# Value products of two heads on the column halves of the array, in an attention, SwiGLU and GELU kernel on one core

## The chip, the core and the metric

The kernel runs on one core of one Trainium2 chip. The metric is the device time of one execution in microseconds (us). TensorE (PE) multiplies, VectorE (DVE), ScalarE (ACT) and GpSimd (POOL) work on tiles, SyncE (SP) issues most transfers. PE multiplies tiles of float32r with one pass over the columns of the moving operand; a float32 product ("exact" here) is issued as one instruction and appears in the trace as two records.

## The reference

Causal attention with a bias from a cumulative sum, then a SwiGLU block and a GELU block (x·sigmoid(1.702x)) on the 2304 tokens.

```
B, H, S, D = 4, 8, 576, 64
scores = q @ k.T / sqrt(D) + min(-(cum_i - cum_j), 0), causal      # cum = cumsum(max(s, 0))
attn = softmax(scores)                                             # sum + 1e-9 below the line
x = (attn @ v) as (2304, 512)
xn = x / sqrt(mean(x*x) + 1e-6) * rms_g
x = (silu(xn @ w_gate) * (xn @ w_val)) @ w_out                     # 512 -> 1536 -> 512
out = gelu(x @ w_in) @ w_out2                                      # 512 -> 2048 -> 512
```

The weights come as 8-byte floats and are decoded on the chip.

## The kernel before

**Attention.** There are 32 heads (4 batches of 8), each with 576 queries and keys in five blocks. `scores` multiplies a head in six pieces of 192, 64, 320, 448, 288 and 288 columns (1600 in all). For the heads in `QF` (0 to 9) each piece is one float32 product of the tiles `QS` and `KS`. For the others the pair of heads is split into high and low halves (`prep`: round, subtract, seven small transfers a head), and each piece is two float32r products (`QA`·`KA`, `QB`·`KB`). DVE adds the mask and takes the row maximum, ACT takes the exponential (`expo`), POOL multiplies by the reciprocal of the row sum (`norm`). `transp` turns the probabilities in four PSUM tiles of 320, 512, 512 and 512 columns; they are copied to the SBUF tiles `PT`. `pv` multiplies them with the values: piece 0 of three products (320, 256, 128 columns), piece 1 of five (four of 256, one of 128), 1856 columns a head.

**The value product.** For the heads in `VF` (0 to 9) `pv` issues one float32 product per part, whose stationary tile `VS` holds the values of both heads of a pair, 128 columns; only the 64 output rows of the head at hand are copied out, to `xT`. For the other 22 heads each of the four `PT` tiles is kept twice, as a rounded copy (`hi`, by ACT) and the rest (`lo`, a DVE subtraction), and each part is two float32r products with a stationary tile of 64 high and 64 low value columns. The two halves of the output are then added (ACT copies one to `BT`, DVE adds).

**What else runs there.** After each batch `rms` takes the row norms: twenty products of a 128-column stationary tile with two columns, then six transposes, of which three have only 64 rows and so use half of the array's rows. Between the heads PE gets "fill": four of the twelve SwiGLU chunks for tokens of batches that are done (`fa_tile`, 256 columns a product, three float32r products for each exact one). When attention ends the rest of SwiGLU and GELU follows, a chain of products of 384 and 512 columns (`Group`, `Down`), to the end.

**The order.** The kernel records all operations, lays them in time with a planner (costs per operation, due times `HD`, `FD`, `WD`, `TA`), lets it choose the engine where an operation names several ("AV": ACT or DVE), and fixes the order on every engine at build time. At run time each engine goes through its list and waits where an input is late. Seven products of no use (`IDLE`) stand at the start.

Of the kernel before, what the change touches and what calls it, by code (L numbers as in the profile page):

```python
# [10 lines left out]
F32 = mybir.dt.float32  # L11
# [12 lines left out]

PRM = {
    "G0": 4, "NWS": 17, "NWO": 12, 
    "QF": set(range(10)), "VF": set(range(10)),
    "TIN": [(t * 256, 256) for t in range(6)],
    "PPB": 3, "PTB": 8, "XHB": 7, "HHB": 5,
    "VIRT": 260096,  # L30
    "SLOTS": {
# [5 lines left out]
    },  # L37
# [8 lines left out]
    "TA": 227.54, "REB": 3, "PASS": 0, "ISSUE": 0.45, "IDLE": 7, "PEN": {},  # L46
}


# [1 line left out]
def attention_then_swiglu_then_gelu(ctx: ExitStack, tc, qT, kT, vp, s, w1, w2, gT, out):  # L51
# [6 lines left out]
    NC2 = w2.shape[0]  # L58
    HB = B * H
    G0 = PRM["G0"]  # L60
    QF, VF = PRM["QF"], PRM["VF"]
    TIN = PRM["TIN"]
    TS = max(n for _, n in TIN)
    TA = sum(n for _, n in TIN)
# [35 lines left out]
    def few(n):  # L100
# [6 lines left out]
    RY = [few(5) for _ in range(2)]  # L107

    SHAPE = {
        "Q": [S], "K": [S], "mask": [S], "SQ": [S], "VS": [5, 2 * D], "PA": [1600], "PT": [512], "VP": [2, 5, 2, D],  # L110
        "BT": [320], "XH": [2, TS], "TH": [TS], "FH": [2, TS], "YO": [2, TS], "w": [2, 512], "wb": [512], "ws": [512],
        "MK": [2, 2, H2], "HH": [2, H2], "M5": [H2], "SG": [H2], "V1": [H2], "RE": [H2], **{nm: [2, 2, H2] for nm in NAMES},
    }
    ROUND = ("QA", "QB", "KA", "KB", "VP", "XH", "FH", "w", "HH", *NAMES)

    def stem(name):
        for k in (name, name[:2], name[:1]):
            if k in SHAPE:
                return k
# [29 lines left out]
    for slot, lists in PRM["SLOTS"].items():  # L149
        k = 0  # L150
        for x, names in enumerate(lists):
            names = names.split()
            if names[0].startswith("PT"):
                if VF:
                    place(slot, k, names, False)
                    k += 1
                place(slot, k, names, True)
            else:
                kind = stem(names[0])
                place(slot, k, names, names[0][:2] in ROUND or kind in ROUND)  # L160
            k += 1
        WIDE[slot] = max(hi - lo for lo, hi, t, _, _ in turns if t == slot)
    starts = [t[0] for t in turns]

    def get(name, n=None):
        if n is None:
            return BUF[name][0]
        return [BUF[f"{name}{i}"][0] for i in range(n)]

    QS, KS, QB, KB, QA, KA, VS, BT, TH = (get(x, 2) for x in ("QS", "KS", "QB", "KB", "QA", "KA", "VS", "BT", "TH"))  # L170
    VTP = get("VP")
    VT = [VTP[:, 0], VTP[:, 1]]
    mask, SQ, SQT, YO = (get(x) for x in ("mask", "SQ", "SQT", "YO"))
    PA = get("PA", NB)
    XH, FH = get("XH", PRM["XHB"]), get("FH", PRM["HHB"])
    PT = {f: [BUF[f"PT{i}"][0 if f else -1] for i in range(PRM["PTB"])] for f in ((True, False) if VF else (False,))}
    WS = [own(f"w{i}", [2, 512], F32R) for i in range(PRM["NWO"])] + [BUF[f"w{i}"][0] for i in range(PRM["NWO"], NWS)]
    PC = {nm: BUF[nm][0] for nm in NAMES}
    MK, HH, M5, SG = get("MK", 2), get("HH", 8), get("M5", 2), get("SG", 2)
# [195 lines left out]
    def sub(o_, x, y, **kw):  # L375
        tt(o_, x, y, ALU.subtract, **kw)
# [21 lines left out]
    def decode(unit, dst):  # L398
        i = unit_i[0]
        unit_i[0] += 1  # L400
        st = ST[i % 2]
        which, c, u = unit
        dma(st, (w1 if which == "1" else w2)[c, :, u, :], after=first_score[:1] if i < 2 else ())
        hw = st.bitcast(I32).rearrange("p (n t) -> p n t", t=2)[:, :, 1]
        lw = st.bitcast(U32).rearrange("p (n t) -> p n t", t=2)[:, :, 0]
        li = st.bitcast(I32).rearrange("p (n t) -> p n t", t=2)[:, :, 0]
        mi, ai = wm.bitcast(I32), dst.bitcast(I32)
        op("A", lambda e: e.activation(out=li, in_=lw, func=AF.Copy, scale=2.0 ** -29), cost=0.68)
        op("V", lambda e: e.tensor_scalar(
            out=mi, in0=hw, scalar1=0x7FFFFFFF, scalar2=None, op0=ALU.bitwise_and), cost=0.43)  # L410
        op("G", lambda e: e.tensor_scalar(
            out=wm, in0=wm, scalar1=E_MAX, scalar2=E_MIN, op0=ALU.min, op1=ALU.max), cost=0.63)
        op("V", lambda e: e.tensor_scalar(
            out=mi, in0=mi, scalar1=3, scalar2=0x3FFFFFFF, op0=ALU.logical_shift_left, op1=ALU.bitwise_and), cost=0.43)
        op("V", lambda e: e.scalar_tensor_tensor(
            out=ai, in0=hw, scalar=-0x40000000, in1=mi, op0=ALU.bitwise_and, op1=ALU.bitwise_or), cost=0.69)
        op("G", lambda e: e.tensor_tensor(out=ai, in0=ai, in1=li, op=ALU.add), cost=1.3)
# [10 lines left out]


    hd = {}  # L430
    pt_i, bt_i, xh_i, fh_i, th_i = [0], [0], [0], [0], [0]

    def turn(bufs, i):
        i[0] += 1
# [53 lines left out]
    def prep(h):  # L488
# [9 lines left out]
        else:  # L498
# [7 lines left out]
            for t, c0, x in ((QA, 0, qh), (KA, 0, kh), (KA, 64, kh), (QA, 64, ql), (QB, 0, qh), (KB, 0, kl)):  # L506
                dma(t[i][c0:c0 + 64, :].bitcast(F32), x)
            dma(KB[i][64:66, :].bitcast(F32), ch_d[h])
        if h not in VF and i == 0:
            src = VS[h // 2 % 2].rearrange("p k (h d) -> p h k d", h=2)  # L510
            rnd(PRM["RV"], VTP[:, :, :, 0, :], src)
            sub(VTP[:, :, :, 1, :], src, VTP[:, :, :, 0, :])

    PO = [576, 640, 832, 1152]

# [54 lines left out]

    def norm(h, qb):
        pt, rc = p_of(h, qb), RC[h % NB]
        op(PRM["NORM"], lambda e: e.tensor_scalar(
            out=pt, in0=pt, scalar1=rc[:, qb:qb + 1], scalar2=1.0, op0=ALU.mult, op1=ALU.mult))

    TP = [
# [7 lines left out]
    def transp(h, t):  # L584
# [8 lines left out]

        op("T", fn)
        n = TCOLS[t]
        hi = turn(PT[h in VF], pt_i)
        if h in VF:
            def fn(e):
                if e.tag == "A":
                    e.activation(out=hi[:, :n], in_=ps[:, :n], func=AF.Copy, scale=1.0)  # L600
                else:
                    e.tensor_copy(out=hi[:, :n], in_=ps[:, :n])

            op("AV", fn)
            hd[h, t] = (hi,)
        else:
            lo = turn(PT[False], pt_i)
            cp(hi[:, :n], ps[:, :n])
            tt(lo[:, :n], ps[:, :n], hi[:, :n], ALU.subtract, eng="V")
            hd[h, t] = (hi, lo)  # L610

    PVP = [
        (0, 320, [(0, 0, 0, 0, 320), (1, 0, 1, 64, 256), (2, 0, 2, 192, 128)]),
# [2 lines left out]
    ]  # L616

    def pv(h, piece, due):
        b_, hh = divmod(h, H)
        f32 = h in VF  # L620
        q0, n, parts = PVP[piece]
        ps = bank(h, "v", 2 * h + piece)
        r0 = 64 * (hh % 2)
        t0 = b_ * S + q0
        xo = xT[r0:r0 + 64, hh // 2, t0:t0 + n]
        for i, (t, c, kb, oc, w) in enumerate(parts):
            def fn(e, i=i, t=t, c=c, kb=kb, oc=oc, w=w):
                if f32:
                    e.matmul(ps[:, oc:oc + w], VS[h // 2 % 2][:, kb, :], hd[h, t][0][:, c:c + w],
                             start=i == 0, stop=i == len(parts) - 1)  # L630
                else:
                    for j in range(2):
                        e.matmul(ps[:, oc:oc + w], VT[h % 2][:, kb].rearrange("p a d -> p (a d)"),
                                 hd[h, t][j][:, c:c + w], start=i == 0 and j == 0, stop=i == len(parts) - 1 and j == 1)

            op("T", fn)
        if f32:
            def fn(e):
                if e.tag == "A":
                    e.activation(out=xo, in_=ps[r0:r0 + 64, :n], func=AF.Copy, scale=1.0)  # L640
                else:
                    e.tensor_copy(out=xo, in_=ps[r0:r0 + 64, :n])

            op("AV", fn, due=due, g=f"h{h}")
            return
        bt = turn(BT, bt_i)
        cp(bt[0:64, :n], ps[64:P, :n])
        tt(xo, ps[0:64, :n], bt[0:64, :n], ALU.add, eng="V", due=due, g=f"h{h}")

# [134 lines left out]
    for h in range(HB):  # L784
# [7 lines left out]
            norm(h, qb)  # L792
        for t in range(4):
            transp(h, t)
        pv(h, 0, PRM["HD"][h])
        pv(h, 1, PRM["HD"][h])
        b_, hh = divmod(h, H)
        if hh % 2:
            rms_sq(b_, hh // 2)
        if hh == H - 1:  # L800
# [326 lines left out]
    n = 0  # L1127
# [322 lines left out]
```

## Time and profile before

| | |
|---|---|
| median of 3 runs | 1039.67 us (1037.95 to 1040.34) |
| the profiled execution, device time | 1040.27 us |
| its span, first to last instruction | 1038.5 us |
| PE busy | 1022.5 us, 98% |
| DVE, ACT, POOL busy | 697.6, 569.3, 407.1 us |
| mean granted clock | 0.995 |

Every instruction has the line L212 of a helper, so the rows are told apart by tiles. A name as `b<-sg,s 128x256` reads: written to PSUM (b), from the moving tile in slot sg and the stationary in slot s, 256 columns. The length of a PE record includes the way through the array and overlaps the next; what an instruction takes from PE is the distance from its start to the next start. The names of slots: sf, sg, sh hold `PT`, sb the split values, s_0_141 the exact `QS` and `KS`.

### The profile page before, as it was taken

To read this page: it belongs to the slowest core of one execution; us is meant where nothing else is said; L and a number is where in the kernel's file an instruction comes from. 1 tells how busy PE (TensorE), PEld (TensorE's weight loads), DVE (VectorE), ACT (ScalarE), POOL (GpSimd) and SP (SyncE) were. 2 spreads that over 40 slices of the span, in tenths; PEclk is the share of its full clock that TensorE was granted. 3 is DMA by queue.
4 is the path that set the end of the run, shared out by engine and by line. 5 is a ranking of instruction groups with operands and counts; after the bars stand their busy time and mean duration, and the time that the engine had idled before them with its cause. 6 is when DMAs were issued, how large, how long until landed. Compare 5 with 4: busy or idle time off the path is not lost.

```text
span 1038.5 us, 17144 instructions
## 1 busy us (share of the span) xinstructions
PE 1022.5 (98%) x6070; PEld 960.2 (92%) x6070; DVE 697.6 (67%) x1573; ACT 569.3 (55%) x1299; POOL 407.1 (39%) x472
## 2 busy tenths in 40 slices
PE   9998999999999999999999999999999999999998
PEld 5877999999999999999999999988999988999987
DVE  6767888877978775787744787876663475473333
ACT  5876786877785445454432444666663344453322
POOL 5666875776563632353300444632330042030000
PEclk9998999999999999999999999999999999999999
DMA  5448665675414745574543277665175136514541
GB/s 153 119 119 198 157 164 148 156 199 139 114 46 132 264 145 190 193 270 157 208 178 122 80 290 279 264 244 233 62 281 196 66 104 255 213 41 158 206 183 61
DMA packets 63037, 176.19 MB, mean 170 GB/s; under 512 B 7220, under 2 KB 24116, under 8 KB 62952
## 3 DMA queue, kind: packets, MB, share of 16 engines
q1 hardware_dynamic: 62840, 175.02, 50.5%
q8 instruction: 48, 0.79, 0.3%
q14 instruction: 37, 0.30, 0.1%
q10 hardware_dynamic: 112, 0.08, 0.0%
HBM read 111.34 MB, written 44.26 MB: 150 GB/s over the span
## 4 chain that ended last, share of the span: by engine, by line
PE 95%; DMA 1%; DVE 1%; SPq 1%; issue 0%; ACT 0%; POOL 0%; DVEq 0%; ACTq 0%
PE b L212 95%; SPq L212 1%; DMA s<-s 1%; DMA s<-in_kT_dram 0%; DVE s L212 0%; DMA s<-in_qT_dram 0%; DVE xT L212 0%; POOL sg L212 0%; DVE sd L212 0%; ACT s L212 0%; ACT sg L212 0%; DVE sh L212 0%; DVE wa L212 0%; ACT sa L212 0%; DVE small L212 0%
## 5 line engine op out<-in xcount | busy, mean ns | idle before, releaser
L212 PE MATMUL b<-s,w 128*128 128x384 f32 x930 | 177.6, 334 | 0.0
L212 PEld LDWEIGHTS b<-s,w 128*128 128x128 f32 x930 | 163.0, 188 | 0.6
L212 POOL TENSOR_TENSOR wa<-wa,st 128x512 int32<-128x512 int32 x52 | 72.9, 1402 | 197.0 <-ACT sb L212 60.8
L212 DVE TENSOR_TENSOR xT<-b,xT 128x384 f32<-128x384 f32 (+1 forms) x134 | 80.3, 609 | 86.5 <-PE b L212 85.5
L212 PE MATMUL b<-sc,w 128*128 128x256 f32 (+1 forms) x744 | 122.5, 301 | 0.0
L212 ACT ACTIVATE b<-b 128x384 f32<-128x384 f32 x119 | 55.8, 480 | 95.8 <-DVE b L212 56.7
L212 PEld LDWEIGHTS b<-sc,w 128*128 128x128 f32 x744 | 106.5, 192 | 0.9 <-issue 0.2
L212 PE MATMUL b<-sd,w 128*128 128x384 f32 (+1 forms) x594 | 107.3, 312 | 0.1
L212 PE MATMUL b<-s 128*128 128x288 f32 (+5 forms) x398 | 92.8, 359 | 7.8 <-DMA s<-in_kT_dram 2.5
L212 POOL TENSOR_SCALAR wm<-wm 128x512 f32<-128x512 f32 x68 | 47.1, 693 | 134.8 <-DVE wm L212 125.8
L212 POOL TENSOR_SCALAR s<-s,small 128x576 f32<-128x576 f32 (+4 forms) x160 | 89.5, 577 | 21.5 <-DVE small L212 10.8
L212 PEld LDWEIGHTS b<-sd,w 128*128 128x128 f32 x594 | 92.7, 189 | 0.8 <-DVE sd L212 0.3
L212 ACT ACTIVATE s<-s,small 128x576 f32<-128x576 f32 (+4 forms) x160 | 88.3, 554 | 7.7 <-DVE small L212 7.2
L212 PE MATMUL b<-s,s 128*128 128x384 f32 (+1 forms) x453 | 91.1, 338 | 0.0
L212 PEld LDWEIGHTS b<-s 128*128 128x128 f32 x398 | 63.0, 198 | 19.3 <-issue 9.0
L212 PEld LDWEIGHTS b<-s,s 128*128 128x128 f32 x453 | 79.6, 188 | 1.2
L212 DVE CUSTOM_DVE_ANT_0 s<-b,s 128x192 f32<-128x192 f32 (+4 forms) x160 | 64.3, 424 | 19.5 <-PE b L212 18.9
L212 PE MATMUL b<-ident,s 128*128 128x128 f32 x480 | 73.1, 277 | 1.3 <-POOL s L212 0.7
L212 PE MATMUL b<-w,sc 128*128 128x512 f32 x270 | 74.2, 390 | 0.0
L212 ACT ACTIVATE sa<-b 128x384 f32<-128x384 f32 (+1 forms) x100 | 45.0, 452 | 47.6 <-DVE b L212 26.9
L212 ACT ACTIVATE se<-b 128x384 f32<-128x384 f32 (+2 forms) x82 | 38.3, 469 | 58.8 <-PE b L212 52.2
L212 ACT ACTIVATE st<-st 128x512 int32<-128x512 uint32 x68 | 45.8, 674 | 40.3 <-DMA st<-in_w_dram 40.0
(152 smaller groups left out, 2183.6 us busy)
## 6 DMA issues: line engine op xcount, KB each, us to landing
st<-in_w_dram SPq DMA_DIRECT2D x68, 512.0 KB
s<-s SPq DMA_DIRECT2D x132, 144.0 KB
s<-pc21B SPq DMA_DIRECT2D x9, 768.0 KB
xT<-y_d SPq DMA_DIRECT2D x3, 1536.0 KB
s<-pc11B SPq DMA_DIRECT2D x6, 768.0 KB
s<-pc22B SPq DMA_DIRECT2D x6, 768.0 KB
out_dram<-xT SPq DMA_DIRECT2D x18, 256.0 KB
s<-in_vp_dram SPq DMA_DIRECT2D x16, 256.0 KB
```

What stands on the lines that cost most here:

```text
L212: return lambda *args, **kw: f(*[real(x) for x in args], **{k: real(x) for k, x in kw.items()})
```

## The change

- `pv` is called once per pair of heads. It issues, for each part, one float32 product for each head, each with 64 value columns, placed on columns 0 to 63 and 64 to 127 of the array (`tile_position`). Both write the same PSUM bank, one the lower, one the upper 64 partitions, and one copy of 128 partitions takes both to `xT`. This goes for all 32 heads; the rounded and rest copies of `PT`, the split of the values (`VP`) and the additions (`BT`) are gone. `PT` has 12 tiles in place of 8.
- `QF` has heads 0 to 13, so four more heads have exact scores.
- The planner may give the normalising to ACT or GpSimd (the table still says GpSimd), and one step of the weight decoding (`mag`) to ACT as well as DVE.
- New due times and a planner's cost for a piece of `pv`.

```
-    "QF": set(range(10)), "VF": set(range(10)),
+    "QF": set(range(14)),
-    "PPB": 3, "PTB": 8, "XHB": 7, "HHB": 5,
+    "PPB": 3, "PTB": 12, "XHB": 7, "HHB": 5,
-    "TA": 227.54, "REB": 3, "PASS": 0, ...
+    "TA": 129.28, "REB": 3, "EARLY": False, "MAG": "AV", "PASS": 0, ..., "PVC": (1.4, 2.1),
...
-        op("V", lambda e: e.tensor_scalar(
-            out=mi, in0=hw, scalar1=0x7FFFFFFF, scalar2=None, op0=ALU.bitwise_and), cost=0.43)
+        def mag(e):
+            if e.tag == "A":
+                e.activation(out=wm, in_=hw.bitcast(F32), func=AF.Abs)
+            else:
+                e.tensor_scalar(out=mi, in0=hw, scalar1=0x7FFFFFFF, scalar2=None, op0=ALU.bitwise_and)
+        op("AV", mag)
...
-        if h in VF:
...
-            op("AV", fn)
-            hd[h, t] = (hi,)
-        else:
-            lo = turn(PT[False], pt_i)
-            cp(hi[:, :n], ps[:, :n])
-            tt(lo[:, :n], ps[:, :n], hi[:, :n], ALU.subtract, eng="V")
-            hd[h, t] = (hi, lo)
+        pt = turn(PT, pt_i)
...
+        op("AV", fn)
+        hd[h, t] = pt
...
-                if f32:
-                    e.matmul(ps[:, oc:oc + w], VS[h // 2 % 2][:, kb, :], hd[h, t][0][:, c:c + w],
-                             start=i == 0, stop=i == len(parts) - 1)
...
+        def fn(e):
+            for i, (t, c, kb, oc, w) in enumerate(parts):
+                for j in range(2):
+                    r0 = 64 * j
+                    e.matmul(ps[r0:r0 + 64, oc:oc + w], VS[h // 2 % 2][:, kb, r0:r0 + 64], hd[h + j, t][:, c:c + w],
+                             start=i == 0, stop=i == len(parts) - 1, tile_position=(0, r0))
+        op("T", fn, cost=PRM["PVC"][piece])
...
-        bt = turn(BT, bt_i)
-        cp(bt[0:64, :n], ps[64:P, :n])
-        tt(xo, ps[0:64, :n], bt[0:64, :n], ALU.add, eng="V", due=due, g=f"h{h}")
...
-        pv(h, 0, PRM["HD"][h])
-        pv(h, 1, PRM["HD"][h])
+        if hh % 2:
+            for piece in range(2):
+                pv(h - 1, piece, PRM["HD"][h // 2])
```

How the order moves, at three places. PE, a piece 0 of the value product among transposes (`ident`) and fill (`sc` by `w`), one of the 22 split heads before:

```order
L212 MATMUL b_69<-ident,s_0_151 128x128 x4
L212 MATMUL b_72<-sc_929,w_130 128x256 x6
L212 MATMUL b_70<-sf_1047,sb_992 128x320 x2
L212 MATMUL b_70<-sf_1047,sb_992 128x256
L212 MATMUL b_70<-sg_1089,sb_992 128x256
L212 MATMUL b_72<-sc_929,w_130 128x256 x3
L212 MATMUL b_70<-sg_1089,sb_992 128x128 x2
```

The same place after, a pair of heads (the slots sa and sb now hold `PT` tiles too):

```order
L204 MATMUL b_69<-ident,s_0_138 128x128 x4
L204 MATMUL b_72<-sc_910,w_129 128x256 x6
L204 MATMUL b_70<-sb_389,s_0_151 64x320
L204 MATMUL b_70<-sf_260,s_0_151 64x320
L204 MATMUL b_70<-sb_389,s_0_151 64x256
L204 MATMUL b_70<-sf_260,s_0_151 64x256
L204 MATMUL b_70<-sb_389,s_0_151 64x128
L204 MATMUL b_70<-sf_260,s_0_151 64x128
```

A piece is now one unbroken stretch of instructions that alternate between the halves; over the whole list there are 256 of them in 31 stretches, with full-array products before and after each.

DVE, before, between the heads of the split kind (the subtractions into sf and sg, the split of the values into sb, the addition of `BT` from sa):

```order
L212 TENSOR_TENSOR sf_1047<-b_68,sf_1047 128x320
L212 SCALAR_TENSOR_TENSOR se_987<-se_987,b_72 128x256
L212 TENSOR_SCALAR sb_992<-s_0_146 128x10x64
L212 TENSOR_TENSOR se_987<-se_987,b_72 128x256
L212 TENSOR_TENSOR sb_992<-s_0_146,sb_992 128x10x64
L212 TENSOR_TENSOR sg_1089<-b_69,sf_1047 128x512
L212 TENSOR_TENSOR xT<-b_70,sa_1127 64x256
L212 TENSOR_TENSOR sg_1089<-b_68,sg_1089 128x512
```

After, at the like place:

```order
L204 SCALAR_TENSOR_TENSOR se_983<-se_983,b_72 128x256
L204 TENSOR_TENSOR se_983<-se_983,b_72 128x256
L204 COPY xT<-b_70 128x320
L204 COPY sf_260<-b_68 128x320
L204 ISA s_0_138,small<-b_66,s_0_147 128x192
L204 ISA small 128x1
```

Copies, shared between DVE and ACT, stand where subtractions, splits and additions stood.

PE at the very start, before (`128x512` are the products of no use, s_0_141 the exact scores):

```order
L212 MATMUL b_72<-s_0_151 128x512 x6
L212 MATMUL b_66<-s_0_141 128x192
L212 MATMUL b_66<-s_0_141 128x64
L212 MATMUL b_73<-s_0_141 128x288
L212 MATMUL b_71<-s_0_141 128x448
```

After:

```order
L204 MATMUL b_72<-s_0_168 128x512
L204 MATMUL b_66<-s_0_141 128x192
L204 MATMUL b_66<-s_0_141 128x64
L204 MATMUL b_73<-s_0_141 128x288
L204 MATMUL b_71<-s_0_141 128x448
L204 MATMUL b_67<-s_0_141 128x320
L204 MATMUL b_66<-s_0_141 128x288
L204 MATMUL b_72<-s_0_168 128x512 x2
```

One product of no use stands ahead of the first head instead of six; the rest are spread between the first heads.

## Rows read from the trace of the kernel before

**Rows 1.** The page: busy time; the granted clock in 40 slices.

```profile
PE 1022.5 (98%) x6070; PEld 960.2 (92%) x6070; DVE 697.6 (67%) x1573; ACT 569.3 (55%) x1299; POOL 407.1 (39%) x472
...
PEclk9998999999999999999999999999999999999999
```

**Rows 2.** Busy time by stretch: start, attention with fill, the chain behind it.

```profile
core 0: us, PE busy (x) PEld busy (x) DVE busy (x) ACT busy (x) POOL busy (x), PEclk, DMA share, GB/s
0.00:100.00 100.00, 91.53 (x466) 71.82 (x467) 68.86 (x238) 67.82 (x191) 63.40 (x99) 0.96 0.54 148
100.00:340.00 240.00, 237.29 (x1893) 231.81 (x1893) 198.46 (x582) 178.59 (x464) 157.45 (x216) 1.00 0.53 140
340.00:1038.50 698.50, 693.63 (x3715) 656.59 (x3713) 430.30 (x755) 322.87 (x646) 186.26 (x158) 1.00 0.50 183
```

**Rows 3.** Waits of PE, longest first: us in total, times, longest.

```profile
PE b L212 <- DMA s<-in_kT_dram: 2.5, 1, 2.5
PE b L212 <- DVE s L212: 2.0, 1, 2.0
PE b L212 <- DMA s<-s: 2.0, 2, 1.3
```

**Rows 4.** Timeline of PE (start, us, operation): exact value product of one head.

```profile
51.26 1.14 PE L212 MATMUL b<-sf,s 128*128 128x320 f32 x4
...
53.96 0.38 PE L212 MATMUL b<-sf,s 128*128 128x128 f32 x2
54.18 0.60 PE L212 MATMUL b<-ident,s 128*128 128x128 f32 x4
54.62 0.39 PE L212 MATMUL b<-sf,s 128*128 128x128 f32 x2
54.84 1.19 PE L212 MATMUL b<-s 128*128 128x288 f32 x4
```

**Rows 5.** Timeline of PE: pieces 0 and 1 of split heads, to the next start.

```profile
149.97 0.58 PE L212 MATMUL b<-sf,sb 128*128 128x320 f32 x3
...
150.50 0.52 PE L212 MATMUL b<-sc,w 128*128 128x256 f32 x3
150.86 0.34 PE L212 MATMUL b<-sg,sb 128*128 128x128 f32 x2
151.04 0.52 PE L212 MATMUL b<-ident,s 128*128 128x128 f32 x3
...
159.25 0.40 PE L212 MATMUL b<-sh,sb 128*128 128x256 f32 x2
...
160.38 0.62 PE L212 MATMUL b<-s 128*128 128x448 f32 x2
160.84 0.88 PE L212 MATMUL b<-sd,w 128*128 128x256 f32 x6
```

**Rows 6.** Timeline of PE: scores of 448 columns of an exact head.

```profile
56.63 0.92 PE L212 MATMUL b<-s 128*128 128x448 f32 x2
57.39 0.60 PE L212 MATMUL b<-ident,s 128*128 128x128 f32 x4
```

**Rows 7.** Timeline of PE: two transposes of 128 rows, one of 64, then fill.

```profile
169.27 0.58 PE L212 MATMUL b<-ident,small 128*128 128x128 f32 x3
169.77 1.33 PE L212 MATMUL b<-sd,w 128*128 128x256 f32 x9
170.94 0.27 PE L212 MATMUL b<-ident,s 128*128 128x128 f32 x1
```

**Rows 8.** Timeline of PE: fill of 256 columns, then norms of two columns.

```profile
162.88 1.60 PE L212 MATMUL b<-sd,w 128*128 128x256 f32 x12
164.32 0.52 PE L212 MATMUL b<-sc,w 128*128 128x256 f32 x3
164.68 1.18 PE L212 MATMUL b<-small,s 128*128 128x2 f32 x10
165.71 0.49 PE L212 MATMUL b<-sd,w 128*128 128x256 f32 x2
```

**Rows 9.** Groups by form, DVE: one of three alike groups of subtractions.

```profile
L212 DVE TENSOR_TENSOR sg<-b,sf 128x512 fp32r<-128x512 f32 x22 | 15.1, 685 | 3.1 <-ACT sf L212 2.8 <-PE b L212 0.3
```

More of the change, by code (lines that the diff above doesn't have):

```diff
@@ L42 @@
            (2, (10, 11)), (1, (10, 11)), (0, (10, 11))],
[3 rows of a table removed]
-    "TA": 227.54, "REB": 3, "PASS": 0, "ISSUE": 0.45, "IDLE": 7, "PEN": {},
[3 rows of a table added]
+    "TA": 129.28, "REB": 3, "EARLY": False, "MAG": "AV", "PASS": 0, "ISSUE": 0.45, "IDLE": 7, "PEN": {}, "PVC": (1.4, 2.1),
 }
@@ L60, in attention_then_swiglu_then_gelu @@
     G0 = PRM["G0"]
-    QF, VF = PRM["QF"], PRM["VF"]
+    QF = PRM["QF"]
     TIN = PRM["TIN"]
@@ L109, in attention_then_swiglu_then_gelu @@
     SHAPE = {
-        "Q": [S], "K": [S], "mask": [S], "SQ": [S], "VS": [5, 2 * D], "PA": [1600], "PT": [512], "VP": [2, 5, 2, D],
-        "BT": [320], "XH": [2, TS], "TH": [TS], "FH": [2, TS], "YO": [2, TS], "w": [2, 512], "wb": [512], "ws": [512],
+        "Q": [S], "K": [S], "mask": [S], "SQ": [S], "VS": [5, 2 * D], "PA": [1600], "PT": [512],
+        "XH": [2, TS], "TH": [TS], "FH": [2, TS], "YO": [2, TS], "w": [2, 512], "wb": [512], "ws": [512],
         "MK": [2, 2, H2], "HH": [2, H2], "M5": [H2], "SG": [H2], "V1": [H2], "RE": [H2], **{nm: [2, 2, H2] for nm in NAMES},
     }
-    ROUND = ("QA", "QB", "KA", "KB", "VP", "XH", "FH", "w", "HH", *NAMES)
+    ROUND = ("QA", "QB", "KA", "KB", "XH", "FH", "w", "HH", *NAMES)
     def stem(name):
@@ L152, in attention_then_swiglu_then_gelu @@
             names = names.split()
[L153 to L157, printed above, removed]
-            else:
-                kind = stem(names[0])
-                place(slot, k, names, names[0][:2] in ROUND or kind in ROUND)
+            kind = stem(names[0])
+            place(slot, k, names, names[0][:2] in ROUND or kind in ROUND)
             k += 1
@@ L168, in get @@
         return [BUF[f"{name}{i}"][0] for i in range(n)]
-    QS, KS, QB, KB, QA, KA, VS, BT, TH = (get(x, 2) for x in ("QS", "KS", "QB", "KB", "QA", "KA", "VS", "BT", "TH"))
-    VTP = get("VP")
-    VT = [VTP[:, 0], VTP[:, 1]]
+    QS, KS, QB, KB, QA, KA, VS, TH = (get(x, 2) for x in ("QS", "KS", "QB", "KB", "QA", "KA", "VS", "TH"))
     mask, SQ, SQT, YO = (get(x) for x in ("mask", "SQ", "SQT", "YO"))
@@ L175, in attention_then_swiglu_then_gelu @@
     XH, FH = get("XH", PRM["XHB"]), get("FH", PRM["HHB"])
-    PT = {f: [BUF[f"PT{i}"][0 if f else -1] for i in range(PRM["PTB"])] for f in ((True, False) if VF else (False,))}
+    PT = get("PT", PRM["PTB"])
     WS = [own(f"w{i}", [2, 512], F32R) for i in range(PRM["NWO"])] + [BUF[f"w{i}"][0] for i in range(PRM["NWO"], NWS)]
@@ L430, in attention_then_swiglu_then_gelu @@
     hd = {}
-    pt_i, bt_i, xh_i, fh_i, th_i = [0], [0], [0], [0], [0]
+    pt_i, xh_i, fh_i, th_i = [0], [0], [0], [0]
     def turn(bufs, i):
@@ L508, in prep @@
             dma(KB[i][64:66, :].bitcast(F32), ch_d[h])
[L509 to L512, printed above, removed]
     PO = [576, 640, 832, 1152]
@@ L572, in norm @@
         pt, rc = p_of(h, qb), RC[h % NB]
-        op(PRM["NORM"], lambda e: e.tensor_scalar(
-            out=pt, in0=pt, scalar1=rc[:, qb:qb + 1], scalar2=1.0, op0=ALU.mult, op1=ALU.mult))
+        def fn(e):
+            if e.tag == "A":
+                e.activation(out=pt, in_=pt, func=AF.Copy, scale=rc[:, qb:qb + 1])
+            else:
+                e.tensor_scalar(out=pt, in0=pt, scalar1=rc[:, qb:qb + 1], scalar2=1.0, op0=ALU.mult, op1=ALU.mult)
+        op(PRM["NORM"], fn)
     TP = [
@@ L595, in transp, with fn @@
         n = TCOLS[t]
-        hi = turn(PT[h in VF], pt_i)
-        if h in VF:
[L598 to L602, printed above, removed]
-            op("AV", fn)
-            hd[h, t] = (hi,)
-        else:
-            lo = turn(PT[False], pt_i)
-            cp(hi[:, :n], ps[:, :n])
-            tt(lo[:, :n], ps[:, :n], hi[:, :n], ALU.subtract, eng="V")
-            hd[h, t] = (hi, lo)
+        pt = turn(PT, pt_i)
+        def fn(e):
+            if e.tag == "A":
+                e.activation(out=pt[:, :n], in_=ps[:, :n], func=AF.Copy, scale=1.0)
+            else:
+                e.tensor_copy(out=pt[:, :n], in_=ps[:, :n])
+        op("AV", fn)
+        hd[h, t] = pt
     PVP = [
@@ L619, in pv, with fn @@
         b_, hh = divmod(h, H)
-        f32 = h in VF
         q0, n, parts = PVP[piece]
         ps = bank(h, "v", 2 * h + piece)
-        r0 = 64 * (hh % 2)
         t0 = b_ * S + q0
-        xo = xT[r0:r0 + 64, hh // 2, t0:t0 + n]
-        for i, (t, c, kb, oc, w) in enumerate(parts):
-            def fn(e, i=i, t=t, c=c, kb=kb, oc=oc, w=w):
-                if f32:
-                    e.matmul(ps[:, oc:oc + w], VS[h // 2 % 2][:, kb, :], hd[h, t][0][:, c:c + w],
-                             start=i == 0, stop=i == len(parts) - 1)
[L631 to L645, printed above, removed]
-        bt = turn(BT, bt_i)
-        cp(bt[0:64, :n], ps[64:P, :n])
-        tt(xo, ps[0:64, :n], bt[0:64, :n], ALU.add, eng="V", due=due, g=f"h{h}")
+        xo = xT[:, hh // 2, t0:t0 + n]
+        def fn(e):
+            for i, (t, c, kb, oc, w) in enumerate(parts):
[4 more added lines that the diff above has]
+        op("T", fn, cost=PRM["PVC"][piece])
+        def fn(e):
+            if e.tag == "A":
+                e.activation(out=xo, in_=ps[:, :n], func=AF.Copy, scale=1.0)
+            else:
+                e.tensor_copy(out=xo, in_=ps[:, :n])
+        op("AV", fn, due=due, g=f"h{h // 2}")
     RO = [0, 128, 256, 384, 448]
```

8 rows, old and new, of the table PRM are left out of this document.

## The prediction

> **What bounds the kernel now.** First the busy times: PE is busy for 1022.5 of 1038.5 us, the next engine, DVE, for 67% [rows 1]. The stretches say where that could differ: in the first 100 us PE has 91.53 busy, from 100 to 340 us, attention with fill, 237.29 of 240, and behind that 693.63 of 698.5, in which nothing of this change lies [rows 2]. DVE has 68.86 + 198.46 = 267 us in the first 340 (79%), ACT 246, POOL 221 [rows 2]: busy, but not the bound. So the change is worth, first, what it takes from or adds to PE's own work in the first 340 us, and second, what becomes of PE's waits there: 8.5 + 2.7 = 11.2 us, of which 2.0 stand before the first instruction and 4.5 are waits for transfers of q and k and of their split copies [rows 2, 3]. The last view is PE's timeline, for prices: since records overlap, a price is the distance to the next start, not the length.
>
> **Value products, before.** An exact head runs from 51.26 to 54.18 and, behind four transposes, from 54.62 to 54.84: 2.92 + 0.22 = 3.14 us for 1856 columns [rows 4]. Ten heads: 31.4 us. A split head has piece 0 from 149.97 to 150.50 and 150.86 to 151.04, 0.71 us, and piece 1 from 159.25 to 160.38, 1.13 us: 1.84 us [rows 5]. Twenty-two heads: 40.5 us. Together 71.9 us.
>
> **Value products, after.** Every part is now an exact product for each head of the pair, with as many columns as before, on its own half of the array. No row shows two halves at work. The ends: the halves run side by side, and a pair costs what one exact head costs, 16 x 3.14 = 50.2 us; or the second half waits for the first, and it costs 100.5 us. I take 50.2. The reason is the alternation of the instructions: the halves share no stationary cells and no PSUM partitions, only the queue, and the queue starts float32r products of 256 columns every 0.12 us (1.44 us for twelve) and products of two columns every 0.103 us (1.03 us for ten) [rows 8], nearly twice as often as an exact record of 256 columns needs (3.14 us over 16 records, the narrow ones among them, is 0.196 each) [rows 4]. So it can hand each half a record in the time of one. The 0.103 us is also a floor per record, if loading 64 stationary columns takes as long as 128: the four records of a 128-column part then need 0.41 in place of 0.22 us, twice a pair, 16 x 2 x 0.19 = 6 us more.
>
> **Going to the halves and back.** The 31 stretches stand among full-array products. The nearest row is a transpose of 64 rows among full ones: the three transposes take 0.50 us from 169.27 to 169.77 [rows 7], while one of 128 rows takes 0.11 (four in 0.44) [rows 4], so that 0.275 were due; the nine fill products behind take 1.17 in place of 9 x 0.12 = 1.08 us [rows 7, 8]. One excursion costs 0.23 + 0.09 = 0.32 us, 31 cost 9.9 us. Those rows halve the rows of the array, not the columns; the ends are 0 and, if column halves cost double, 20. I take 9.9, the row's value. Value products: 50.2 + 9.9 - 71.9 = -11.8 us.
>
> **Scores.** An exact piece of 448 columns takes 0.76 us (56.63 to 57.39) [rows 6], a split one 0.46 (160.38 to 160.84) [rows 5]: 0.30 us more, over 1600 columns 1.07 us a head, for heads 10 to 13 +4.3 us. Their rounding, their subtractions and seven transfers a head go; these hang on SP and DMA, beside PE.
>
> **Waits of PE.** DVE loses the subtractions of `lo`: one group of 22 is 15.1 us [rows 9], there are three alike and a narrower fourth, so over 45 of 267 us; the additions of `BT` and ACT's copies for them go as well, and the split of the values. In return some copies of `PT` and a step of the decoding may move to either engine. So PE's suppliers are less loaded in the stretch from 100 us on. Before 100 us PE's share per exact head falls by half a value product, so the same work of ACT, POOL and DVE must keep up with a faster PE; they stand at 63 to 69% there [rows 2], and have room for it. Of the 9.2 us of waits behind the start, 4.5 are for transfers, which a lighter DVE does not bring earlier; of the other 4.7 I let half go: -2.4 us. Ends: -9 (all gone) and +9 (as much again). At the start one product of no use runs ahead of the first scores where six did; the first head may start sooner, but on a clock not yet raised. At half the clock its scores take 0.76 x 1600 / 448 = 2.7 us more [rows 6]; against the fillers no longer waited for I take nothing, +-2.7 at most.
>
> **The sum,** against the profiled execution: 1040.27 - 11.8 + 4.3 - 2.4 = 1030.4 us; that execution is 0.6 us above the median of 1039.67. Forecast: **1030 us**. The chain behind 340 us, its order and its one visible weakness (4.9 us without PE busy) are taken as unchanged.
>
> **Rivals.**
> 1. *The halves take turns.* Each half's product starts when the other ends: 100.5 in place of 50.2, 1030 + 50 = **1080 us**, slower. For it: nothing in the trace shows two products in the array at once. Against it: what stands above on the queue. It decides once more than 11 of the 50 us of overlap are lost, a pair over 3.14 + 0.7 = 3.8 us, excursions apart. Chance 0.12.
> 2. *Loads stand in the open.* The value columns of both heads reach over the same 128 rows. If a load into one half could not run beside a product in the other, then on top of the first rival 512 loads of half of 0.103 us are added, 26 us: **1106 us**. Against it: from 100 to 340 us loads are busy for 231.81 beside 237.29 of products over the same 128 rows [rows 2], so they run beside each other on the full array. Chance 0.03. The Trainium skill, "TensorE: Matmul & The Clock Gate", Part 3, says that a load overlaps products in flight only where its row group differs, which would give this rival; the trace of the full array does not agree with it in that form.
> 3. *The overlap is partial.* The floor of 0.103 us a record holds: +6, **1036 us**, still under the kernel before. Chance 0.12. The Trainium skill, "TensorE: Matmul & The Clock Gate", Part 3, gives 2.38 times for three column tiles, 79% of the ideal; that is an estimate of 63 us for the value products here, which alone would put the time at 1043 us, and no run here shows it.
> 4. *Waits eat the gain.* A pair's product needs the eight `PT` tiles of both heads, and there are twelve; while the second head's chain (scores, exponential on ACT, normalising on POOL, transposes, copies) is late, PE stands, and behind it in its list the transposes and scores of the next heads. One such wait of the size of the longest in the trace, 2.5 us [rows 3], at every fourth or fifth pair gives +11: **1041 us**, no change. For it: the product comes later than one head's did, and POOL is alone with the normalising. Against it: the room on all three engines, and fill in PE's list from the middle of attention on. It decides from 0.6 us a pair. Chance 0.13.
> 5. Forecast, 0.60, with 1018 to 1037 as its own range (excursions free, or waits up).
>
> **Range and chances.** A measurement of this kernel tells about 0.2%, 2.1 us, from no change: faster is under 1037.6, slower over 1041.8. Faster: 0.60, of the third rival 0.08, of the fourth 0.02: 0.70. Same: 0.04 and 0.05: 0.09. Slower: 0.06 of the fourth, 0.15 of the first two: 0.21. For the range the first two rivals are left out, 0.15, and 0.05 at the edges: low 1015, where excursions cost nothing (-9.9) and most of the other waits go (-5); high 1046, where the floor (+6) and the upper end of the waits (+9 and a little) come together.
>
> **What the profile after would show.** The 64-column products: if a part of 256 columns for both heads takes 0.43 us from start to start, the halves are side by side; 0.87 is the first rival, more the second, 0.41 for a part of 128 the third. The first fill or transposes behind a stretch: 0.3 us more in all than their own time, or nothing. PE busy in the first 340 us falls by some 8 us and attention ends that much earlier, or, in the fourth rival, the waits of PE grow beyond 20 us with POOL or ACT as the releaser, while the products are as cheap as forecast. DVE's 697.6 us fall by 45 or more, to no direct use [rows 1, 9]. The forecast is wrong if the halves do not overlap, and, with them overlapped, if the waits of the first 340 us rise by 10 us.

## The result

The changed kernel takes 1024.16 us (median of 4 runs, 1023.57 to 1025.08) beside 1039.41 us (4 runs) for the kernel before: a ratio of 0.9855, 95% interval 0.9838 to 0.9872, 15 us less. The forecast was 1030 us, with 1015 to 1046 as its range: the direction held, and so did the price of the products that it rests on; the gain came out half as large again as the 9.9 us that the sum gave (-11.8 + 4.3 - 2.4).

The page of the changed kernel, its busy times and the clock, for [rows 1]:

```profile
PE 1006.5 (98%) x6070; PEld 922.1 (90%) x6070; DVE 628.7 (61%) x1437; ACT 562.4 (55%) x1271; POOL 361.2 (35%) x442
...
PEclk9999999999999999999999999999999999999999
```

Its stretches, for [rows 2] (us of the stretch, then busy us of PE, PEld, DVE, ACT, POOL, the granted clock, DMA):

```profile
0.00:100.00 100.00, 92.39 (x555) 66.25 (x557) 72.14 (x261) 74.75 (x205) 69.07 (x113) 1.00 0.45 130
100.00:340.00 240.00, 236.78 (x1898) 215.24 (x1895) 159.69 (x484) 154.09 (x401) 124.61 (x181) 1.00 0.56 155
340.00:1022.00 682.00, 677.36 (x3623) 640.61 (x3621) 396.89 (x694) 333.51 (x668) 167.52 (x149) 1.00 0.50 180
```

And PE's waits, for [rows 3]:

```profile
PE b L204 <- DVE s L204: 5.8, 1, 5.8
PE b L204 <- DVE small L204: 1.9, 2, 1.4
PE b L204 <- DMA s<-s: 1.8, 2, 1.2
...
PE b L204 <- DMA s<-in_kT_dram: 0.4, 1, 0.4
```

PE is busy 16 us less, in as many records, and 98% of a shorter span. The dip of the clock in the fourth slice of [rows 1] is gone: from 78 to 104 us the granted clock was 0.80, now it is 1.00. Attention's last transpose starts at 321.3 us in place of 337.8, so the gain is made in attention and none behind it. PE's waits in the first 340 us are 7.6 + 3.2 = 10.8 us against 11.2, but 5.8 of them (2.0 before) now stand ahead of PE's first instruction, which is a product of no use in both kernels: behind the start they fell from 9.1 to 5.0.

The timeline of PE through one piece 1 of a pair (start, us, operation; `128*64` is a product on half of the columns), with the fill and transposes around it:

```profile
189.30 0.52 PE L204 MATMUL b<-sc,w 128*128 128x256 f32 x3
189.75 0.43 PE L204 MATMUL b<-sg,s 128*64 128x256 f32 x1
189.76 0.43 PE L204 MATMUL b<-sh,s 128*64 128x256 f32 x1
190.02 0.38 PE L204 MATMUL b<-sg,s 128*64 128x256 f32 x1
190.02 0.38 PE L204 MATMUL b<-sh,s 128*64 128x256 f32 x1
190.23 0.38 PE L204 MATMUL b<-sf,s 128*64 128x256 f32 x1
190.24 0.38 PE L204 MATMUL b<-sg,s 128*64 128x256 f32 x1
...
191.53 0.27 PE L204 MATMUL b<-sf,s 128*64 128x128 f32 x1
191.53 0.27 PE L204 MATMUL b<-sh,s 128*64 128x128 f32 x1
191.64 0.27 PE L204 MATMUL b<-sf,s 128*64 128x128 f32 x1
191.64 0.27 PE L204 MATMUL b<-sh,s 128*64 128x128 f32 x1
191.85 0.62 PE L204 MATMUL b<-sd,w 128*128 128x256 f32 x3
192.31 0.60 PE L204 MATMUL b<-ident,s 128*128 128x128 f32 x4
```

Every record of one head starts within 0.01 us of its partner of the other head (5 to 8 ns over all 256 pairs). From 190.02 to 190.23 both heads get a record of 256 columns, 0.21 us. Before, one head got one in that time, two from 52.24 to 52.67, out of the stretch of [rows 4]:

```profile
52.24 0.59 PE L212 MATMUL b<-sg,s 128*128 128x256 f32 x2
52.67 1.03 PE L212 MATMUL b<-sf,s 128*128 128x256 f32 x4
```

The narrow records come every 0.11 us in pairs, so the 0.103 us is no floor for two halves. What a stretch costs beyond its columns stands at its seams: the three fill products ahead take 0.45 us in place of 0.36, the first pair 0.27 in place of 0.21, the last 0.21 in place of 0.11, the three fill products behind 0.46 in place of 0.36.

### The profile page after: what moved, and what is told of

The parts are those of the page before. It is cut to its first block, busy times and chain, and to the rows that moved or that the text cites. A ratio compares the mean times of both kernels' runs of the same rounds, so it can differ in the third digit from the quotient of the medians.

```text
span 1022.8 us, 16837 instructions
## 1 busy us (share of the span) xinstructions
PE 1006.5 (98%) x6070; PEld 922.1 (90%) x6070; DVE 628.7 (61%) x1437; ACT 562.4 (55%) x1271; POOL 361.2 (35%) x442
## 4 chain that ended last, share of the span: by engine, by line
PE 95%; DVE 2%; DMA 1%; POOL 0%; ACT 0%; issue 0%; POOLq 0%; DVEq 0%; ACTq 0%; SPq 0%
PE b L204 95%; DMA s<-s 1%; DVE xT L204 1%; DVE s L204 0%; DMA s<-in_kT_dram 0%; DMA y_d<-se 0%; ACT s L204 0%; POOL sg L204 0%; DMA s<-in_s_dram 0%; ACT sg L204 0%; POOL wa L204 0%; DVE wm L204 0%; DVE b L204 0%; DVE sa L204 0%; POOL s L204 0%
## 5 line engine op out<-in xcount | busy, mean ns | idle before, releaser
L204 PE MATMUL b<-sc,w 128*128 128x256 f32 (+1 forms) x744 | 125.8, 301 | 0.0
L204 PE MATMUL b<-sd,w 128*128 128x384 f32 (+1 forms) x594 | 110.6, 313 | 0.0
L204 PE MATMUL b<-s 128*128 128x288 f32 (+5 forms) x398 | 96.4, 367 | 9.9 <-DVE s L204 5.8
L204 ACT ACTIVATE s<-s,small 128x192 f32<-128x192 f32 (+4 forms) x160 | 88.1, 554 | 6.9 <-DVE small L204 5.7
L204 POOL TENSOR_SCALAR wm<-wm 128x512 f32<-128x512 f32 x68 | 44.4, 652 | 98.3 <-ACT wm L204 53.7
L204 PEld LDWEIGHTS b<-ident,s 128*128 128x128 f32 x480 | 55.5, 141 | 9.2 <-issue 4.3
```

What stands on the lines that cost most here:

```text
L204: return lambda *args, **kw: f(*[real(x) for x in args], **{k: real(x) for k, x in kw.items()})
```

## The experiments

The times are medians beside runs of the kernel before on the same chip; ratios are to the kernel before. "Loss" is, here and below, my own sum over the 6070 PE records of one traced execution: the distance from start to start, less what the same form takes in an undisturbed row. It counts waits, a low clock and seams alike, also where the page shows PE busy: a record of 384 columns is 0.33 us long, and the next starts 0.17 us behind its start, so the first 0.16 us of a wait are hidden under a record. Which row counts as undisturbed moves such a sum by about 1 us where it is small and by up to 5 us where it is large.

**Halves in turn.**

```
-            for i, (t, c, kb, oc, w) in enumerate(parts):
-                for j in range(2):
+            for j in range(2):
+                for i, (t, c, kb, oc, w) in enumerate(parts):
```

> The changed kernel with one loop turned round: a piece issues all products of the first head, then all of the second, on the same halves. Theory (the halves run side by side because neighbours in PE's list lie on different halves; products on one half run one after another): the overlap goes but for the seam, the stretches grow from 54.8 us in all to about 100, the time from 1024 to about 1069 us, and the parts of 256 columns read 0.43 us a head. Rival (the queue looks far enough ahead to start the second head's products beside the first's, whatever the order): no change, 1024 us.

1052.62 us, ratio 1.0127 (1.0105 to 1.0149): 28 us more than the changed kernel, and neither theory. The stretches take 85.2 us in all, 30 us more. A piece 1 in the timeline of PE; head one's products are sa, sb, sb, sa, sb in the list, then head two's sg, sf, sf, sg, sf:

```profile
45.81 0.65 PE L204 MATMUL b<-sa,s 128*64 128x256 f32 x2
46.29 1.03 PE L204 MATMUL b<-sb,s 128*64 128x256 f32 x4
47.16 0.38 PE L204 MATMUL b<-sa,s 128*64 128x256 f32 x1
47.16 0.43 PE L204 MATMUL b<-sg,s 128*64 128x256 f32 x1
47.37 0.38 PE L204 MATMUL b<-sa,s 128*64 128x256 f32 x1
47.43 0.38 PE L204 MATMUL b<-sg,s 128*64 128x256 f32 x1
47.59 0.27 PE L204 MATMUL b<-sb,s 128*64 128x128 f32 x1
47.65 0.38 PE L204 MATMUL b<-sf,s 128*64 128x256 f32 x1
47.70 0.27 PE L204 MATMUL b<-sb,s 128*64 128x128 f32 x1
47.86 0.81 PE L204 MATMUL b<-sf,s 128*64 128x256 f32 x3
```

Head two's first record starts at 47.16, ahead of three records of head one that stand before it in the list (47.37, 47.59, 47.70). So PE does start a record ahead of earlier ones that wait for their own half, but over three records only, in each of the 31 stretches; the six records before them ran alone here. The alternation in `pv` carries most of the overlap, some 30 of its 50 us.

**The price of an excursion.** One idle exact product of 64 columns on the full array, at the end of each piece, then in its middle. The lines that are new in the second run (in the first the product stands behind the loop):

```
+                if i == len(parts) // 2:
+                    e.matmul(ps[:, 384:448], VS[h // 2 % 2][:, 1, :], hd[h, 1][:, 0:64], start=False, stop=False, skip_group_check=True)
```

> The changed kernel with one idle exact product of 64 columns on the full array (its output goes to unused columns of the bank) at the END of each of the 32 pieces. It is the counterpart of the next run: both theories expect 32 times about 0.22 us, +7 us, about 1031 us.

> The same idle product in the MIDDLE of each piece, so that PE leaves the halves and comes back once more per piece. Theory (each way out and back costs about 0.32 us, as the rows of the 64-row transposes say): 32 x 0.32 = 10 us over the run with the product at the end, about 1041 us. Rival (what the stretches take above the columns' time is the filling of the two halves at their start alone, or nothing): the same as the run before, 1031 us.

1030.58 us (0.9922, 0.9899 to 0.9945) and 1040.28 us (1.0011, 1.0002 to 1.0021): 9.7 us apart, as the theory had it (10): 0.30 us for each of 32 ways out and back. In the timeline of the second, the idle product (`sf` by `s`, 64 columns on the full array) stands alone between two products on the halves:

```profile
31.20 0.38 PE L204 MATMUL b<-sf,s 128*64 128x256 f32 x1
31.21 0.38 PE L204 MATMUL b<-sh,s 128*64 128x256 f32 x1
31.52 0.43 PE L204 MATMUL b<-sf,s 128*128 128x64 f32 x2
31.88 0.43 PE L204 MATMUL b<-sg,s 128*64 128x256 f32 x1
31.89 0.43 PE L204 MATMUL b<-sh,s 128*64 128x256 f32 x1
32.15 0.38 PE L204 MATMUL b<-sg,s 128*64 128x256 f32 x1
```

The record ahead takes 0.32 us in place of 0.21, the two idle ones 0.36 in place of about 0.22, the first behind 0.27. The Trainium skill, "TensorEngine Tiling (Array Packing)", Tiling Modes, says that a change of the tiling mode drains the engine; it gives no time. The rows above, at 0.32, 0.36 and 0.27 us, agree with it, and the two runs give 0.30 us for the way out and back together.

**Exact scores for ten heads instead of fourteen**, in the changed kernel, and for fourteen instead of ten in the kernel before:

```
-    "QF": set(range(14)),
+    "QF": set(range(10)),
```

> The changed kernel with exact scores for heads 0 to 9 only, as before the change. Theory (scores are a plain price on PE, 1.07 us a head by the rows of before): -4.3 us, about 1020 us, with PE's waits unchanged. Rival (the four exact heads pay for themselves, since two more split pairs bring 28 transfers, roundings and subtractions, which PE waits for): 1024 us or more, with the waits of PE on transfers of split copies grown.

> The kernel before with one part of the change alone: exact scores for heads 0 to 13 in place of 0 to 9, due times as before. Theory (the split heads' transfers are what PE waits for at the turn from exact to split heads, between 60 and 100 us, where fill has not begun; moving the turn back saves these waits): the four heads cost 4.3 us on PE, the waits of the first 100 us and the clock lost with them fall by as much or more, time 1030 to 1040 us. Rival (a plain price, as the prediction had it): +4.3 us, about 1044 us.

The first: 1043.01 us (1.0043, 1.0028 to 1.0058), 19 us more than the changed kernel though PE has less to do: the rival, and by far. The loss between 60 and 100 us is 18.7 us, in the changed kernel 4.3. PE's longest entry in the list of waits is now the split copies, 1.8 us in the changed kernel:

```profile
PE b L204 <- DMA s<-s: 9.5, 4, 5.4
```

Its timeline of PE at the turn from exact to split heads (idle time before a row in brackets, with what ended it):

```profile
72.86 0.33 PE L204 MATMUL b<-s 128*128 128x192 f32 x1 [1.59 <-DMA s<-s]
78.61 1.76 PE L204 MATMUL b<-s 128*128 128x192 f32 x5 [5.42 <-DMA s<-s]
80.17 2.13 PE L204 MATMUL b<-small,s 128*128 128x2 f32 x10
82.16 2.06 PE L204 MATMUL b<-s 128*128 128x320 f32 x8
...
92.41 0.72 PE L204 MATMUL b<-ident,small 64*128 64x64 f32 x3 [2.34 <-DVE xT L204]
93.06 1.08 PE L204 MATMUL b<-sc,w 128*128 128x256 f32 x6
93.94 0.36 PE L204 MATMUL b<-s 128*128 128x192 f32 x1
96.16 0.82 PE L204 MATMUL b<-s 128*128 128x192 f32 x3 [1.86 <-DMA s<-s]
```

The first split head's scores stand at 72.86 and 78.61 and wait for the transfers of the split copies; the first fill product comes at 93.06. So PE has nothing to do meanwhile, and behind the wait of 5.42 us the ten norm products take 1.99 us where [rows 8] has 1.03. The granted clock there is 0.50, the lower of its two levels (us of the stretch, busy us of PE, granted clock, DMA):

```profile
80.17:82.16 1.99, 1.99 (x12) 0.50 1.15 276
```

In the changed kernel fill starts before the turn:

```profile
89.15 0.60 PE L204 MATMUL b<-sc,w 128*128 128x256 f32 x3
...
105.82 0.60 PE L204 MATMUL b<-sc,w 128*128 128x256 f32 x3
106.25 0.25 PE L204 MATMUL b<-s 128*128 128x192 f32 x1
107.69 0.52 PE L204 MATMUL b<-s 128*128 128x192 f32 x3 [1.19 <-DMA s<-s]
```

Fill at 89.15, the first split scores at 106.25 and 107.69, one wait of 1.19 us. Exact heads need no splitting and no transfers from SBUF to SBUF; four more of them move the turn behind the end of batch 0, where fill begins. Up to 54 us PE's order is that of the changed kernel; behind that the planner laid the rest anew, and an order with an earlier fill might save a part of the 19 us, which no run tries.

The second, in the kernel before: 1048.78 us (1.0079, 1.0056 to 1.0102), 9 us slower: here my theory fell, and the plain price of the rival (+4.3) is too small as well. The loss between 60 and 100 us did go down, from 10.2 to 4.1 us, as expected, but the four heads' price came on top and the loss between 100 and 350 us went up from 7.5 to 16.9. Which part of that is these heads and which an order that doesn't fit them, this run doesn't tell.

**The value products alone:** the changed kernel with ten exact heads, the due times of before and the decoding step on DVE.

> The value products alone: the changed kernel with exact scores for heads 0 to 9, the due times of the kernel before (for a pair, its second head's) and the decoding step on DVE. Theory (the products are worth 15 us on PE whatever else is there, but PE, being faster, comes earlier to the turn to split heads and waits there): PE's own work falls by 15 us, its waits in the first 100 us grow by 5 to 15, time 1027 to 1036 us. Rival (PE's saving comes through in full): 1024 us or less, since the four exact heads' 4.3 us are saved as well.

1046.89 us (1.0075, 1.0048 to 1.0102): slower than the kernel before, beyond both theories. PE's own work is some 22 us less by the same sum, but the loss between 60 and 100 us is 18.5 us (10.2 before), and between 100 and 350 us 21.2 (7.5, and about 6 us of seams are due).

**Old due times**, of fill, first weights and chain, in the changed kernel; no operation changes, only the order:

> The changed kernel with the due times of fill, of the first weights and of the chain as they were before (the heads keep their new ones). Theory (the place of fill in PE's list beside the turn to split heads is what holds PE's waits down; the old due times put it elsewhere): 5 to 15 us more, 1029 to 1039 us, with PE's loss grown between 60 and 350 us. Rival (the order is good enough with any due times, the exact heads 10 to 13 do it alone): 1024 us, within 2.

1035.81 us (0.9974, 0.9951 to 0.9997): 11.7 us more, the theory. The loss between 60 and 100 us stays low (6.2), so the exact heads do that part by themselves; the rest is lost between 150 and 250 us, 17.5 in place of 6.2 us. The trace shows more loss than the median has: it is of an execution of 1040.42 us, with a granted clock of 0.95 in that stretch (1.00 in the changed kernel), while two of the five executions, with a mean clock of 1.000, took 1033.73 and 1034.80. Its list of PE's waits has nothing large, but much that is small:

```profile
PE b L204 <- DVE s L204: 5.9, 1, 5.9
PE b L204 <- DVE small L204: 3.3, 5, 1.3
PE b L204 <- issue: 3.0, 1, 3.0
PE b L204 <- DMA s<-ch_d: 1.7, 1, 1.7
PE b L204 <- POOL s L204: 1.5, 1, 1.5
```

**The planner's price of a piece,** 1.5 and 2.25 us in place of 1.4 and 2.1; again only the order changes:

> The changed kernel with nothing but the planner's price of the two pieces of a value product changed, from 1.4 and 2.1 to 1.5 and 2.25 us, about what a stretch takes from the product before it to the one behind it in the trace of the changed kernel. No operation changes; the order does. Theory (the order as such is worth 5 to 12 us, and the one on record sits near the best of what its due times can give): slower by 3 to 12 us, 1027 to 1036 us, with PE's own work the same to 1 us and all of the difference in its waits. Rival (small shifts of the order cost nothing, so that what the other runs lost is the load that each put on): 1024 us, within 2, or less since the price is nearer to the truth.

1027.67 us (0.9889, 0.987 to 0.9907), at the edge of what can be told from the changed kernel: 3.5 us more. Together the two say that order alone moves this kernel by up to 12 us; a run that changes an operation carries such a share too, since the planner lays everything anew.

**DVE's load put back, the decoding step back on DVE, normalising on two engines.**

```
+        if h > 9:
+            op("V", lambda e: e.tensor_copy(out=pt[:, :n], in_=ps[:, :n]))
```

> The changed kernel with DVE's load put back: for heads 10 to 31 each PT tile is copied a second time, by DVE from PSUM, the same values, 88 instructions of 0.48 to 0.69 us, about 56 us of DVE, in the place where the subtractions were. Theory (the lighter DVE had little part in it, since PE's waits lay at the turn to split heads): within 2 us of the changed kernel, at most 1026 us. Rival (the relief of DVE and the shorter way from PSUM to PT is what brought PE's waits down by 8 us): 1030 us or more.

> The changed kernel with the moved decoding step back on DVE for all 68 units (51 are on ACT now): 26 us of DVE more, 30 us of ACT less, some 15 units of it before the end of attention. Theory (DVE's load decides PE's waits in attention, as the doubled copies showed with 56 us): 2 to 5 us more, 1026 to 1029 us. Rival (a step off the way from scores to value products hides in DVE's idle time): 1024 us, within 2.

> The changed kernel with normalising allowed on ACT as well as GpSimd. Theory (POOL alone with it costs PE next to nothing, since PE's waits on POOL's normalising are 0.2 us in the changed kernel's list of waits): 1024 us, within 3, either way by the order alone. Rival (POOL's 90 us of normalising stand on the way from scores to transposes; shared, heads come through sooner): 1020 us or less.

1038.94 us (0.9982, 0.9965 to 0.9999), 1030.50 us (0.9918, 0.9903 to 0.9933) and 1030.96 us (0.992, 0.9906 to 0.9935). The doubled copies cost 15 us, 3 us more than order alone did in any run: the rival by its number. Their loss sits between 60 and 80 us (4.8 us, 1.4 in the changed kernel) and between 100 and 150 (10.0 against 3.3). That it is DVE's 56 us is likely and not shown: the longer way from PSUM to `PT` comes with them, and PE's order departs further from the changed kernel's than in any other run here that keeps the products. Of the 2478 records of its first 345 us 1812 stand in the same sequence, with old due times 1958, with the planner's price 2175 (my count). The decoding step (+6) and the shared normalising (+7) came out above both of their theories, and inside what order can do; neither is settled.

**The start.** In the changed kernel PE starts at 5.85 us, and the first scores run at half rate: the two records of 448 columns take from 9.90 to 11.40, 1.49 us where [rows 6] has 0.76. (The profile's records of the clock begin at 12.18 us, with the full clock, so the page's row of the clock doesn't show this.) With the idle products first again:

```
-        op("V", lambda e: e.memset(PA[2][:, 0:512], 1.0))
+        op("V", lambda e: e.memset(PA[2][:, 0:512], 1.0), due=-1000.0)
```

> The changed kernel with the seven products of no use first again, as in the kernel before (the fill of their operand is given the earliest due time). In the changed kernel PE's first instruction stands at 5.85 us in place of 2.04, and the first head's scores run at half the clock. Theory (that start costs what it looks like): PE starts at 2 us, the scores of head 0 at full clock, 2 to 3 us less, about 1021.5 us. Rival (the first scores wait for q, k and the cumulative sum anyway, and the first transposes for the normalising on POOL): no change, 1023 to 1025 us.

1024.53 us (0.9851, 0.9829 to 0.9872), the same as the changed kernel. PE's first instruction moves from 5.85 to 1.45 us, but it is a product of no use in both. The first scores start at 9.20 us, behind all the idle products, and end at 12.00, at full rate; in the changed kernel they start at 7.75 and end at 12.81. The first transposes come at 18.64 us in place of 20.77, the first value products at 27.85 in place of 31.54. This lead is lost again in attention, by order or by what follows; the rival holds for the time, its reason is not shown.

## Why the prediction was right, point by point

- **Value products after: right.** 60.1 us forecast. The stretches take 54.8 us from start to start, and 5.3 us more lie in the records just ahead and behind: 60.1. Side by side was right (first and third rival out), and so was the size of an excursion, 0.32 us from the 64-row transposes against 0.30 us measured.
- **Value products before: close.** I had 71.9 us from one head of each kind; summed over all their records they take 31.1 + 44.2 = 75.2 us. Of the difference 3.0 us belong to the transposes ahead (37 float32r records behind them read 0.08 us longer, the last transpose as much shorter). So this part gave 12.1 us, or 15.1 by the plain sum, where 11.8 was forecast.
- **Scores: right as a price, wrong as a whole.** By the median distance of each form a head takes 2.81 us exact and 1.69 split in the changed kernel, so four heads cost 4.5 us, against +4.3. (All score records together, waits and half rate included, went from 73.9 to 77.4 us.) But the rest of the step, splitting and transfers "beside PE", failed: they are beside PE only where PE has other work. With ten exact heads the changed kernel waits for them at the turn, and loses 19 us.
- **Waits: right sign, too small, for a reason I had denied.** I let half of 4.7 us go and kept the 4.5 us for transfers. Behind the start the waits fell by 4.1 us, 2.1 of it the wait for k (2.5 to 0.4), and the low clock of the first 100 us went with them (0.96 to 1.00). All PE time that is neither value products (the 75.2 and 60.1 us above) nor scores fell by some 7.6 us. The later turn has a part in it (ten exact heads), the order another (old due times), a lighter DVE perhaps a third (doubled copies); they are not additive, and how the 5 us of gain beyond the forecast divide stays open.
- **The start: "nothing" was about right.** As the prediction had it, the first scores start sooner and run slower: at 7.75 us in place of 9.54, and for 5.06 us in place of 2.81 (2.3 us more, 2.7 forecast), so that they end at 12.81 in place of 12.35. The first transposes come 2.3 us later (20.77, before 18.43), inside the 2.7 that I allowed. The 3.8 us by which PE's first instruction moved concern a product of no use. That the time doesn't feel the start is luck as far as is known: the run with the old start leads by 2 to 4 us and ends with no gain.
- **Rivals.** The second (loads in the open) fell: two halves with a load for each record keep to the columns' time, 0.21 us for a pair of 256 columns over the same 128 rows. The Trainium skill's rule on row groups ("TensorE: Matmul & The Clock Gate", Part 3) does not hold here for column halves. The fourth was nearer than its 0.13 suggests: all seven runs with the same cheap products and another order in attention (old due times, doubled copies, ten exact heads, value products alone, planner's price, decoding step, normalising) take 3 to 23 us more than the changed kernel. The largest of their waits is another than the rival named: split copies on their way at the turn, 5.42 us with ten exact heads, and not a pair's `PT` tiles. That the gain came through whole is so in part luck of the forecast: the change came with an order that fits it, for which the sum had no term; with the old order and ten exact heads the same products gave 1046.89 us.

## What to carry to other kernels

Two exact products with 64 value columns each, on the two column halves, took the time of one here (0.21 us a pair of 256 columns), as long as they alternate in the list; count 0.3 us for every stretch of them among full-array products. An engine's saved work is worth its time only while there is something behind it. Where stages with their own transfers begin, look whether other work is in the list by then, and if not, a dearer form that needs no transfers can be the cheaper one. And in a kernel whose order is planned, run the order alone as a control (other due times, nothing else) before a run that drops one part is read as that part's price.

## What the runs showed that was not expected

- Products on different column halves start out of the list's order: a record of head two ran ahead of three records of head one (47.16 against 47.37, 47.59 and 47.70 us), and so in every stretch of that run.
- Neighbours on the two halves start 5 to 8 ns apart. The Trainium skill, "TensorE: Matmul & The Clock Gate", Part 3, gives about 4 ns for each further tile; the trace is close to it.
